# Attention scores in two fp32r parts, issued as pairs on the two row halves of the array

## The chip, the core and the metric

The kernel runs on one core of a Trainium2 chip. TensorE (PE; its weight loads appear as PEld) multiplies, VectorE (DVE), ScalarE (ACT) and GpSimd (POOL) work on the results, SyncE (SP) and ScalarE issue DMAs. The metric is the device time of one execution in microseconds; lower is better.

## The reference

Two layers, each used twice in turn, on x of 2048 rows by 512 columns: A is a Fourier mixing layer (two real DFTs as matmuls), B an attention in four segments of 512 positions with a running memory. B is where the change lies. Cut to what matters:

```python
q, k, v = x @ wq, x @ wk, x @ wv          # 32 heads of 16, segments of L = 512
for s in range(4):
    logits = einsum("bhqd,bhkd->bhqk", qs, ks) * scale + mask   # causal
    p = softmax(logits); a_dot = einsum("bhqk,bhkd->bhqd", p, vs)
    a_mem = (phi(qs) @ M) / (phi(qs) @ z + 1e-6)
    o = g * a_mem + (1 - g) * a_dot
    M, z = M + phi(ks).T @ vs, z + sum(phi(ks))
return concat(o) @ wo
```

## The kernel before, in words

The whole program is placed by hand on a line of slots: `place(order, generator, times)` puts one step of a generator into a slot, and a loop at the end runs the slots in order, within a slot by `order`. PE's matmuls keep that order on the chip. Times in slots, `t` for a unit's start.

**A unit** is four heads (HU) of one segment; a segment has eight, an attention 32, the program 64, and a unit's slots begin ten after those of the one ahead. One unit goes through these steps:

- `proj` (four slots, per group of eight heads) multiplies queries or keys into the bank `pqk` and splits them into parts, so that products of parts come near fp32. Before: three bf16 parts, by one ACT copy out of the bank, a POOL cast (L763), a POOL subtraction (L764), an ACT copy (L768) and a POOL subtraction (L772). Parts go by SP's queue (L781) to a scratch in DRAM, in six slots per head, so that query slot times key slot sums the six products of parts that matter.
- `stack` (slot t - 21) loads the slots of four heads back (L803), 96 rows high: `stkq` and `stkk`, with three more rows for the maxima (ones on the key side).
- `natural_max` (ten slots from t - 17) computes scores with queries on the partitions into banks called `nat` (L819 by way of the helper L82), one head at a time, 96 rows deep. DVE adds the mask and takes each row's maximum (L832). Four small DVE operations (L848 to L855) split the maxima into three bf16 parts.
- `max_rows` (slot t - 4): PE transposes the parts into the bank `mT`, ACT copies them out (`mt`, L870) and issues a DMA (L871) that writes them into the three extra rows of `stkq`.
- `softmax_values` (13 slots from t): the scores again, this time keys on the partitions and less the maxima, 99 rows deep, into banks `sT`. ACT clamps the diagonal (L900) and takes the exponential (L901) into `pT`; POOL zeroes what is above the diagonal (L904). In slot t + 12 the values are multiplied (`pv_bank`): four heads side by side on four column tiles of the array, 17 columns each.
- `output` (slot t + 14) transposes (`on`) and divides.

Score matmuls have 512, 384, 256 or 128 columns because of causality; per unit there are four of each for `nat` and four of each for `sT`. In every slot of the ten stand one bank of `sT` and one of `nat`, 512 columns each, and behind them in the same slot a step of a projection (`pqk`, `pvv`, `po`), of the memory (`pkT`, `pM`, `pm`) or a transpose. There are eight banks, one of which `pv_bank` keeps.

The other matmuls are fp32r with both operands split in two (`matmul3`), 128 rows by 512 columns, or plain fp32 (`pv`, `pM`, `pm`, which appear as two passes, and the transposes). PE loads weights for the next matmul while one runs.

The functions that the change touches:

Of the kernel before, what the change touches and what calls it, by code (L numbers as in the profile page):

```python
# [10 lines left out]
F32 = mybir.dt.float32  # L11
F32R = mybir.dt.float32r
# [44 lines left out]
def spectral_infini_kernel(  # L57
# [111 lines left out]
    def finish(ps, xr, x_out, i):  # L169
# [8 lines left out]
        consts.tile([P, MCOPIES, HU, LT], BF16, name=f"mparts{i}") for i in range(2)  # L178
# [500 lines left out]
    def place_attention(x_in, x_out, t0, w_at, out_at):  # L679
# [49 lines left out]
        def proj(s, g, n):  # L729
# [17 lines left out]
            parts = sb.tile([P, 3, 512], BF16, name="parts", bufs=2)  # L747
            with_phi = (n == "q" and s > 0) or (n == "k" and s < NSEG - 1)
            late = s == 0 and g < 2
            rem = sb.tile([P, 512], F32, name="rem", bufs=1)  # L750
            raw = sb.tile([P, 512], F32, name="praw", bufs=2) if with_phi else rem
# [11 lines left out]
            G.tensor_copy(parts[:, 0], raw)  # L763
            G.tensor_tensor(out=rem, in0=raw, in1=parts[:, 0], op=ALU.subtract)  # L764
# [3 lines left out]
            A.activation(parts[:, 1], rem, AF.Copy)  # L768
# [3 lines left out]
            G.tensor_tensor(out=parts[:, 2], in0=rem, in1=parts[:, 1], op=ALU.subtract)  # L772
# [3 lines left out]
            o = 0  # L776
            for a, cnt, step in SLOTS[n]:
                src = parts[:, a : a + cnt] if step else parts[:, a : a + 1].to_broadcast(
                    [P, cnt, 512]
                )  # L780
                nc.sync.dma_start(dst[:, o : o + cnt], src)  # L781
                o += cnt
# [7 lines left out]
        def stack(s, g, u):  # L790
            for n in "qk":
                number = (s * NG + g) * (HG // HU) + u
                if n == "q" or number < 3:
                    t = sb.tile(
                        [P, HU, 512], BF16, name=f"stk{n}", tag={"q": "chi", "k": "clo"}[n], bufs=3
                    )
                if n == "k" and number < 3:
                    G.memset(t[KROWS : KROWS + MROWS], 1.0)
# [11 lines left out]
        def natural_max(s, g, u):  # L810
# [3 lines left out]
            def scores(*cols):  # L814
                ps = bank("nat")
                views, off = [], 0
                for h, i in cols:
                    n = (i + 1) * P
                    T.matmul(  # L819
                        ps[:, off : off + n],  # L820
                        qs[:KROWS, h, i * P : (i + 1) * P],
                        ks[:KROWS, h, :n],
                        start=True,
                        stop=True,
                    )
                    views.append((ps[:, off : off + n], mx[:, h, i : i + 1]))
                    off += n
                for src, dst in views:
# [17 lines left out]
            rem = sb.tile([P, HU, LT], F32, name="mrem", bufs=2)  # L846
            with tc.high_priority(offset=2 * URGENT):
                V.scalar_tensor_tensor(  # L848
                    parts[:, 0], mx, -2.0, mx, op0=ALU.mult, op1=ALU.add
                )  # L850
                for dst in rem, parts[:, 1]:
                    V.scalar_tensor_tensor(
                        dst, mx, -1.0, parts[:, 0], op0=ALU.mult, op1=ALU.subtract
                    )
                V.scalar_tensor_tensor(  # L855
                    parts[:, 2], rem, 1.0, parts[:, 1], op0=ALU.mult, op1=ALU.subtract
                )
# [3 lines left out]
        def max_rows(s, g, u):  # L861
            qs, parts = stacks[s, g, u, "q"], maxima.pop((s, g, u))
            pt = bank("mT", (P, 2 * 512), BF16)
            T.transpose(
                pt[: MCOPIES * HU * LT, :P], parts.rearrange("p a h i -> p (a h i)"), ident_b
            )
            n = MROWS * HU * LT
            mt = sb.tile([P, P], BF16, name="mt", bufs=2)
            with tc.high_priority(offset=URGENT):
                A.activation(mt[:n], pt[:n, :P], AF.Copy)  # L870
            nc.scalar.dma_start(  # L871
                qs[KROWS : KROWS + MROWS].rearrange("p h s -> p (h s)"), mt[:n]
            )
            yield

        def softmax_values(s, g, u):
# [4 lines left out]
            def scores(dst, *cols):  # L881
                ps = bank("sT")
                off, diag = 0, []
                for h, kt in cols:
                    n = 512 - kt * P
                    T.matmul(
                        ps[:, off : off + n],
                        ks[:K, h, kt * P : (kt + 1) * P],
                        qs[:K, h, kt * P :],
                        start=True,  # L890
                        stop=True,
                    )
                    diag.append(off // P)
                    off += n
                blocks = ps.rearrange("p (b c) -> p b c", c=P)
                blocks = blocks[:, diag[0] : diag[-1] + 1 : max(1, diag[-1] - diag[0])]
                if x_out is out_tiles and (s * NG + g) * NU + u >= NSEG * USEG - 3 and cols[0][0] % 2:
                    V.tensor_scalar_max(blocks, blocks, 0.0)
                else:
# [442 lines left out]
```

## Time and profile before

| what | value |
|---|---|
| median of 3 runs | 1798.72 us (1797.68 to 1799.42) |
| span of the profiled execution | 1798.4 us |
| PE busy | 1742.2 us (97%) |
| DVE, ACT, POOL busy | 1405.3, 1110.9, 471.9 us |
| mean granted TensorE clock | 0.996 |
| attention stages | about 430 to 910 us and 1320 to 1798 us |

A row of a group gives the line, the engine, the operation, what is written and read, partitions by elements, the count, then busy time, the mean duration of one in ns, and the engine's idle time ahead of it with what ended it. A timeline row gives start and length in us. A matmul's length is from its start to its modelled end and overlaps with the next one; what PE needs for one is read from start to start. An fp32 matmul and its weight load are one instruction of the program, but appear as two in the trace.

### The profile page before, as it was taken

The numbers are of one execution on the slowest core, as the hardware profiler recorded it, in microseconds if no ns is written. First come the engines' busy times: TensorE is split into PE (matmuls) and PEld (weight loads), VectorE is DVE, ScalarE is ACT, GpSimd is POOL, SyncE is SP. The second block draws the span as 40 slices with busy tenths as digits, with TensorE's granted clock in tenths as the row PEclk, the third lists the DMA queues.
The fourth block names the chain that finished last, engine by engine and source line by source line (L and its number), as shares of the span: only waits on it lengthen the run. The fifth ranks groups of instructions, "written<-read, shape, count | busy, mean of one in ns | idle before, by whom it ended". The sixth has DMA issues, their size and how long they took to land.

```text
span 1798.4 us, 32155 instructions
## 1 busy us (share of the span) xinstructions
PE 1742.2 (97%) x10192; PEld 1257.4 (70%) x10192; DVE 1405.3 (78%) x4242; ACT 1110.9 (62%) x2391; POOL 471.9 (26%) x789
## 2 busy tenths in 40 slices
PE   8999999999999999998999999999998999999998
PEld 6888777877556666665568888888875666666654
DVE  8888978764887878877877997667658778787785
ACT  3344443432787878787773666444428887877785
POOL 1000000003453445454420000000134443544442
PEclk9999999999999999999999999999999999999999
DMA  8787775355453444433566777644546435344341
GB/s 289 239 277 236 250 230 170 113 166 169 142 161 109 156 128 129 150 116 122 165 199 213 265 231 238 195 154 142 167 143 185 129 118 160 117 145 140 104 131 42
DMA packets 169498, 302.81 MB, mean 168 GB/s; under 512 B 19568, under 2 KB 70768, under 8 KB 169328
## 3 DMA queue, kind: packets, MB, share of 16 engines
q1 hardware_dynamic: 159152, 287.39, 50.2%
q10 hardware_dynamic: 10176, 13.37, 2.1%
q8 instruction: 80, 1.31, 0.3%
q14 instruction: 90, 0.74, 0.1%
HBM read 211.83 MB, written 88.08 MB: 167 GB/s over the span
## 4 chain that ended last, share of the span: by engine, by line
PE 72%; DVE 11%; issue 2%; ACT 2%; DMA 1%; ACTq 0%; POOL 0%; DVEq 0%; SPq 0%
PE m L82 20%; PE pqk L82 9%; PE y L82 8%; PE pv_bank L82 8%; PE sT L82 7%; PE nat L82 6%; PE po L82 4%; PE pvv L82 4%; DVE junk L832 4%; DVE c L522 1%; PE pM L82 1%; PE pm L82 1%; PE on L82 1%; DVE clo L98 1%; ACT pT L901 1%
## 5 line engine op out<-in xcount | busy, mean ns | idle before, releaser
L832 DVE CUSTOM_DVE_ANT_0 junk<-nat,mask 128x512 bf16<-128x512 f32 (+3 forms) x1024 | 496.0, 484 | 143.2 <-PE nat L82 108.3
L901 ACT ACTIVATE pT<-sT 128x512 f32<-128x512 f32 x640 | 372.3, 599 | 18.1 <-ACT sT L900 4.7
L904 POOL TENSOR_SCALAR_AFFINE_SELECT pT<-pT 128x256 f32<-128x256 f32 (+1 forms) x448 | 201.8, 464 | 476.1 <-ACT pT L901 364.7
L82 PE MATMUL m<-chi,xa 128*128 128x512 f32 x1056 | 308.9, 393 | 2.9 <-DVE c L522 2.1
L82 PE MATMUL nat<-stkk,stkq 96*128 96x512 bf16 (+3 forms) x1024 | 244.5, 300 | 8.4 <-DVE mx L832 4.7
L82 PE MATMUL sT<-stkq,stkk 99*128 99x256 bf16 (+3 forms) x1024 | 248.8, 305 | 3.4 <-ACT pT L901 1.2
L900 ACT ACTIVATE sT<-sT 128x256 f32<-128x256 f32 (+1 forms) x628 | 205.2, 336 | 52.7 <-PE sT L82 47.2
L82 PE MATMUL m<-clo,xa 128*128 128x512 f32 x720 | 232.0, 394 | 5.1 <-DVE clo L98 5.1
L82 PEld LDWEIGHTS m<-chi,xa 128*128 128x128 f32 x1056 | 198.2, 188 | 46.0 <-DVE c L522 2.9
L82 PE MATMUL y<-wdt,us 128*128 128x512 f32 x768 | 182.3, 391 | 0.2 <-DVE wdt L98 0.2
L82 PEld LDWEIGHTS <-stkk 99*128 99x128 bf16 x1024 | 80.9, 98 | 134.2 <-issue 122.4
L82 PEld LDWEIGHTS y<-wdt,us 128*128 128x128 f32 x768 | 143.4, 188 | 30.5 <-DVE wdt L98 0.9
L82 PEld LDWEIGHTS m<-clo,xa 128*128 128x128 f32 x720 | 135.1, 188 | 37.3 <-DVE clo L98 9.6
L82 PE MATMUL pv_bank<-pT,v_all 128*17 128x512 f32 (+3 forms) x2048 | 153.6, 438 | 0.0
L96 ACT ACTIVATE chi<-cring 128x512 fp32r<-128x512 f32 (+1 forms) x138 | 99.6, 727 | 86.8 <-PE m L82 34.5
L145 POOL TENSOR_TENSOR r<-ve,half_neg 128x2 f32<-128x2 f32 (+2 forms) x24 | 19.3, 806 | 475.3 <-DVE ve L143 471.8
L82 PEld LDWEIGHTS <-stkq 96*128 96x128 bf16 x1024 | 94.1, 99 | 61.2 <-issue 20.2
L82 PE MATMUL pvv<-wv,xT 128*128 128x512 f32 x384 | 126.3, 440 | 3.7 <-DVE mx L832 3.7
L82 PE MATMUL pqk<-xT,wq 128*128 128x512 f32 x384 | 127.8, 442 | 0.0
L82 PE MATMUL po<-wo,oh 128*128 128x512 f32 x384 | 122.7, 435 | 0.9 <-ACT oh L96 0.5
L82 PE MATMUL pqk<-xT,wk 128*128 128x512 f32 x384 | 123.2, 430 | 0.0
L82 PEld LDWEIGHTS pv_bank<-pT,v_all 128*17 128x17 f32 x2048 | 54.0, 98 | 87.2 <-issue 83.0
(195 smaller groups left out, 2987.3 us busy)
## 6 DMA issues: line engine op xcount, KB each, us to landing
cring<-in_ct SPq DMA_DIRECT2D x97, 256.0 KB
stkq<-scrq SPq DMA_DIRECT2D x64, 384.0 KB
stkk<-scrk SPq DMA_DIRECT2D x64, 384.0 KB
cring<-sum SPq DMA_DIRECT2D x95, 256.0 KB
xt<-mid SPq DMA_DIRECT2D x64, 256.0 KB
cring<-in_ct SPq DMA_DIRECT2D x27, 512.0 KB
mid<-xr SPq DMA_DIRECT2D x48, 256.0 KB
scrq<-parts SPq DMA_DIRECT2D x32, 384.0 KB
```

Of the source, the lines that this page charges most:

```text
L82: return tc.keep_in_program_order(op(*args, **kwargs))
L96: pin(A.activation(hi, src, AF.Copy, scale=scale))
L98: lo_engine.tensor_tensor(out=lo, in0=src, in1=hi.bitcast(F32), op=ALU.subtract)
L145: G.tensor_tensor(out=r, in0=ve, in1=half_neg[:, :n], op=ALU.pow)
L522: V.tensor_tensor(out=dst, in0=c[tcn, base][:, m], in1=ps[m], op=op)
L832: last_max[0] = V.tensor_tensor_reduce(junk[:, :n], src, mask[:, 512 - n :], 1.0, 3e38, ALU.add, ALU.min, dst,)
L900: A.activation(blocks, blocks, AF.Relu)
L901: A.activation(dst, ps, AF.Exp, scale=-SCALE)
L904: G.affine_select(blocks, blocks, pattern=[[0, n] for n in blocks.shape[1:-1]] + [[1, P]], compare_op=ALU.is_ge, fill=0.0, base=0, channel ...
```

## The change

Queries and keys are split into two fp32r parts (the rounded value and the rest) and not three bf16 parts: three slots per head in the scratch, 48 rows in place of 96, and two rows of maxima in place of three, so 50 in place of 99. A stack now holds two heads in partitions 0 to 63 and two in 64 to 127. A score matmul of a head in the lower half and the same one of a head in the upper half are issued one behind the other, into two banks. The compiled program gives them a tile of 64 rows by 128 columns at row 0 and at row 64.

`natural_max` runs in five slots, two apart, in place of ten; `softmax_values` puts its `sT` pairs into the same five (t, t + 2, ... t + 8). So in every second slot stands a burst of four `sT` matmuls (or two of 512 columns) and as many `nat`, and in the slots between there are no scores. The last `nat` burst stands at t - 10 (before t - 8), the step on the maxima stays a slot or more behind (t - 8, before t - 7), `max_rows` stays at t - 4, `stack` moves to t - 22.

The first cut of the diff has the constants (a slot list now has part, first slot, count) and the splitting:

```diff
-SLOTS = {"q": ((0, 3, 0), (1, 2, 0), (2, 1, 0)), "k": ((0, 3, 1), (0, 2, 1), (0, 1, 1))}
-NSLOT = 6
+SLOTS = {"q": ((0, 0, 2), (1, 2, 1)), "k": ((0, 0, 1), (1, 1, 1), (0, 2, 1))}
+NSLOT = 3
 KROWS = NSLOT * DH
-MROWS = 3
+MROWS = 2
+SIDES = (0, 64)
+HP = 2
...
             A.activation(raw, ps, AF.Copy, scale=sign)
-            G.tensor_copy(parts[:, 0], raw)
-            G.tensor_tensor(out=rem, in0=raw, in1=parts[:, 0], op=ALU.subtract)
+            A.activation(parts[:, 0], ps, AF.Copy, scale=sign)
+            G.tensor_tensor(out=parts[:, 1], in0=raw, in1=parts[:, 0].bitcast(F32), op=ALU.subtract)
...
-            A.activation(parts[:, 1], rem, AF.Copy)
...
-            G.tensor_tensor(out=parts[:, 2], in0=rem, in1=parts[:, 1], op=ALU.subtract)
-            yield
-            sd = dram.tile([NSLOT, P, 512], BF16, name=f"scr{n}", bufs=3)
+            yield
+            sd = dram.tile([NSLOT, P, 512], F32, name=f"scr{n}", bufs=3)
```

The stacks, the scores for the maxima and the maxima:

```diff
-                last_stack[0] = nc.sync.dma_start(
-                    t[:KROWS].rearrange("p h s -> p (h s)"),
-                    src[:, u * HU * 512 : (u + 1) * HU * 512],
-                )
+                for a, at in enumerate(SIDES):
+                    first = (u * HU + a * HP) * 512
+                    last_stack[0] = nc.sync.dma_start(
+                        t[at : at + KROWS].rearrange("p h s -> p (h s)").bitcast(F32),
+                        src[:, first : first + HP * 512],
+                    )
...
             def scores(*cols):
-                ps = bank("nat")
+                banks = [bank("nat") for _ in SIDES]
                 views, off = [], 0
-                for h, i in cols:
+                for p, i in cols:
                     n = (i + 1) * P
-                    T.matmul(
-                        ps[:, off : off + n],
-                        qs[:KROWS, h, i * P : (i + 1) * P],
-                        ks[:KROWS, h, :n],
+                    for a, at in enumerate(SIDES):
+                        T.matmul(
+                            banks[a][:, off : off + n],
+                            qs[at : at + KROWS, p, i * P : (i + 1) * P],
+                            ks[at : at + KROWS, p, :n],
...
-            for h in range(HU):
-                scores((h, 3))
+            for p in range(HP):
+                scores((p, 3))
                 yield
-                scores((h, 0), (h, 2))
+                scores((p, 0), (p, 2))
                 yield
-                if h % 2:
-                    scores((h - 1, 1), (h, 1))
-                    yield
+            scores((0, 1), (1, 1))
+            yield
...
+                V.tensor_scalar(parts[:, 0], mx, -1.0, None, op0=ALU.mult)
                 V.scalar_tensor_tensor(
-                    parts[:, 0], mx, -2.0, mx, op0=ALU.mult, op1=ALU.add
-                )
-                for dst in rem, parts[:, 1]:
-                    V.scalar_tensor_tensor(
-                        dst, mx, -1.0, parts[:, 0], op0=ALU.mult, op1=ALU.subtract
-                    )
-                V.scalar_tensor_tensor(
-                    parts[:, 2], rem, 1.0, parts[:, 1], op0=ALU.mult, op1=ALU.subtract
+                    parts[:, 1], mx, -1.0, parts[:, 0].bitcast(F32), op0=ALU.mult, op1=ALU.subtract
                 )
...
-            nc.scalar.dma_start(
-                qs[KROWS : KROWS + MROWS].rearrange("p h s -> p (h s)"), mt[:n]
-            )
+            for a, at in enumerate(SIDES):
+                for r in range(MROWS):
+                    j = (r * HU + a * HP) * LT
+                    nc.scalar.dma_start(
+                        qs[at + KROWS + r : at + KROWS + r + 1].rearrange("p h s -> p (h s)").bitcast(F32),
+                        mt[j : j + HP * LT].bitcast(F32),
+                    )
```

`softmax_values` is changed in the same way (two banks, a loop over SIDES inside that over the columns, then clamp and exponential for each bank), with its three kinds of bursts at these slots, and the placement of the steps:

```diff
-                ev(6 + h, first)
+                ev(6 + 2 * p, first)
-                ev(2 + h, second)
+                ev(2 + 2 * p, second)
-                ev(h // 2, third)
+            ev(0, third)
...
-            place(1, natural_max(*unit(n)), run_from(t - 17, 10), [t - 7])
-            place(0.5, stack(*unit(n)), [t - 21])
+            place(1, natural_max(*unit(n)), run_from(t - 18, 5, 2), [t - 8])
+            place(0.5, stack(*unit(n)), [t - 22])
```

How this moves PE's instructions: here is PE before, from the end of one unit's values on (`stkk` and `stkq` are the stacks, `pm` reads the memory, `pqk` is a projection).

```order
L82 MATMUL pv_bank<-pT,v_all 17x512 x4
L82 MATMUL pv_bank<-pT,v_all 17x384 x4
L82 MATMUL pv_bank<-pT,v_all 17x128 x4
L82 MATMUL pv_bank<-pT_20107,v_all 17x256 x4
L82 LDWEIGHTS stkk
L82 MATMUL sT<-stkq,stkk 128x384
L82 LDWEIGHTS stkk
L82 MATMUL sT<-stkq,stkk 128x128
L82 LDWEIGHTS stkq
L82 MATMUL nat<-stkk,stkq 128x256
L82 LDWEIGHTS stkq
L82 MATMUL nat<-stkk,stkq 128x256
```

And PE after, at the same place:

```order
L84 MATMUL pv_bank<-pT,v_all 17x512 x4
L84 MATMUL pv_bank<-pT,v_all 17x384 x4
L84 MATMUL pv_bank<-pT,v_all 17x128 x4
L84 MATMUL pv_bank<-pT_18669,v_all 17x256 x4
L84 MATMUL sT<-stkq,stkk 128x384 x2
L84 MATMUL sT<-stkq,stkk 128x128 x2
L84 MATMUL nat<-stkk,stkq 128x512 x2
L84 MATMUL pm<-state_15711,phi 128x136 x2
L84 MATMUL pqk<-xT,wq 128x512 x3
L84 MATMUL sT<-stkq,stkk 128x384 x2
L84 MATMUL sT<-stkq,stkk 128x128 x2
L84 MATMUL nat<-stkk,stkq 128x128 x2
```

The weight loads of the scores are no longer instructions of their own, each score matmul has its partner behind it, and the projection that stood in every slot now stands between two bursts. Over the whole program the matmuls change between the array's three shapes (whole, 128 rows by 32 columns for `pv_bank`, 64 rows by 128 columns) 724 times, before 128 times.

The second place is ACT around the maxima of a unit. Before:

```order
L900 ACTIVATE sT<-sT 128x128
L870 ACTIVATE mt<-mT 48x128
L901 ACTIVATE pT<-sT 128x512
L871 DMA stkq<-mt 3x16x128
L900 ACTIVATE sT<-sT 128x128
L901 ACTIVATE pT<-sT 128x512
```

After:

```order
L900 ACTIVATE sT<-sT 128x128 x2
L864 ACTIVATE mt<-mT 32x128
L901 ACTIVATE pT<-sT 128x512 x2
L868 DMA stkq<-mt 1x8x128 x4
L900 ACTIVATE sT<-sT 128x128 x2
L901 ACTIVATE pT<-sT 128x512 x2
```

One issue of a DMA has become four, and ACT handles the banks of a pair together: two clamps, then two exponentials.

More of the change, by code (lines that the diff above doesn't have):

```diff
@@ L177, in spectral_infini_kernel @@
     max_parts = [
-        consts.tile([P, MCOPIES, HU, LT], BF16, name=f"mparts{i}") for i in range(2)
+        consts.tile([P, MCOPIES, HU, LT], F32R, name=f"mparts{i}") for i in range(2)
     ]
@@ L969, in last @@
                 pv(pb, 3, p1, 384)
-                pv(pb, 2, (p2[0][:, :2], p2[0][:, 2:]), 0)
+                pv(pb, 2, [p2[0][:, :, p] for p in range(HP)], 0)
                 ot = sb.tile([P, 512], F32, name="ot", tag="ut", bufs=8)
@@ L1287, in setup @@
         yield
-    ident = ident_b = mask = same_head = gate = None
+    ident = mask = same_head = gate = None
     def ones():
```

119 lines of the change are left out of this document (56 added, 63 removed).

## The prediction

> **What bounds the kernel now.** I read the page first: busy times, then the granted clock (full speed in all forty slices).
>
> ```profile
> span 1798.4 us, 32155 instructions
> PE 1742.2 (97%) x10192; PEld 1257.4 (70%) x10192; DVE 1405.3 (78%) x4242; ACT 1110.9 (62%) x2391; POOL 471.9 (26%) x789
> ```
>
> TensorE (PE) is busy for 97% of the span. Since the change touches only the attention stages, I read the busy time by windows there next: two stretches in the middle of an attention and two at an end.
>
> ```profile
> 600.00:700.00 100.00, 98.64 (x705) 64.04 (x707) 83.24 (x347) 79.39 (x188) 46.46 (x82) 1.00 0.42 134
> 1500.00:1600.00 100.00, 98.33 (x699) 64.04 (x698) 82.64 (x342) 81.52 (x195) 50.85 (x87) 1.00 0.40 124
> 800.00:880.00 80.00, 73.33 (x539) 44.30 (x537) 65.64 (x268) 62.13 (x148) 40.40 (x69) 0.96 0.47 147
> 1700.00:1798.40 98.40, 89.25 (x666) 53.16 (x664) 68.72 (x285) 67.66 (x161) 33.06 (x70) 1.00 0.28 87
> ```
>
> The columns are PE, PEld (weight loads), DVE, ACT and POOL. In the middle PE leaves 1.5 us of 100 free; DVE and ACT follow with about 83 and 80. At the ends PE waits for 7 to 9 us. So in most of the attention a microsecond of PE is a microsecond of time, and the question is what the new score matmuls cost PE, switching included.
>
> The profiled execution's span, 1798.4, is 0.3 us under the median of the runs, 1798.72, so the sum is made against the span and stands for both.
>
> **What the scores cost now.** The timeline of PE around two slots, and one long piece of the critical chain for the price of an ordinary fp32r matmul:
>
> ```profile
> 1225.46 31.96 PE y L82 x141
> 606.53 0.38 PE L82 MATMUL sT<-stkq,stkk 99*128 99x512 bf16 x1
> 606.75 0.38 PE L82 MATMUL nat<-stkk,stkq 96*128 96x512 bf16 x1
> 606.78 1.05 PE L82 MATMUL po<-wo,oh 128*128 128x512 f32 x3
> 610.21 0.39 PE L82 MATMUL sT<-stkq,stkk 99*128 99x256 bf16 x2
> 610.44 0.38 PE L82 MATMUL nat<-stkk,stkq 96*128 96x512 bf16 x1
> 610.47 1.04 PE L82 MATMUL pqk<-xT,wq 128*128 128x512 f32 x3
> 612.27 0.40 PE L82 MATMUL pqk<-xT,wq 128*128 128x512 f32 x1
> ```
>
> An fp32r matmul of 512 columns follows the next every 31.96/141 = 0.227 us. Three of them last 2 x 0.227 + 0.40 = 0.85. The three po end at 607.83, so without the scores they would have begun at 606.98: the scores in front of them took 606.98 - 606.53 = 0.45. The same for the second slot: 611.51 - 0.85 - 610.21 = 0.45; with about 0.01 for the hand-over from fp32r to bf16, 0.46 for 1024 columns. A unit (four heads) has ten such slots, 4.60 us, and there are 64 units: 294 us of PE time.
>
> **The pairs.** After the change two matmuls, on array rows 0-63 and 64-127, are issued one behind the other. What the trace has of tiles side by side is pv: four column tiles.
>
> ```profile
> 612.60 0.62 PE L82 MATMUL pv_bank<-pT,v_all 128*17 128x512 f32 x4
> 614.33 0.61 PE L82 MATMUL pv_bank<-pT,v_all 128*17 128x256 f32 x8
> 607.68 1.09 PE L82 MATMUL pM<-v_all,pkn 128*128 128x136 f32 x8
> 608.60 0.28 PE L82 MATMUL pm<-state,phi 128*128 128x136 f32 x1
> ```
>
> Four pv matmuls lie within 0.62, barely more than one, so a further tile costs some 0.007. No row shows row tiles, nor fp32r narrower than 512. I take pairs that run together, 0.22/512 us a column (sT to nat above), and 0.227 at 512: 0.234 for 512 columns, 0.179 for 384, 0.124 for 256. For 128 columns the stream would be 0.07, but each matmul needs its own fp32 weight load; eight pM matmuls with a load each, 0.28 long like the pm behind them, show a pace of (1.09 - 0.28)/7 = 0.116, so 0.116. A unit has four pairs of each width: 4 x 0.653 = 2.61 us. Saved: 64 x (4.60 - 2.61) = 127 us. Bounds: if the 128-column pair took twice its load (about what two fp32 passes of that width take, by the pace of pM), +0.116 x 4 x 64 = +30; if the load came faster, -0.05 x 4 x 64 = -13.
>
> **The switches.** These take it back. Entering and leaving a tiled mode:
>
> ```profile
> 612.60 0.13 PEld L82 LDWEIGHTS pv_bank<-pT,v_all 128*17 128x17 f32 x7 [0.37 <-issue]
> 931.08 0.40 PE L82 MATMUL pv_bank<-pT,v_all 128*17 128x256 f32 x4
> 931.40 0.50 PE L82 MATMUL m<-chi,xa 128*128 128x512 f32 x1
> 931.40 0.19 PEld L82 LDWEIGHTS m<-chi,xa 128*128 128x128 f32 x1 [0.42 <-issue]
> ```
>
> Into pv: the last pqk started at 612.27, pv at 612.60, 0.33 later where 0.227 is usual: 0.10 lost, and pv's load begins only then. Out of pv: the last group starts at 931.08, m at 931.40, 0.32 where the two groups at 614.33 are 0.61 - 0.40 = 0.21 apart: 0.11 lost. Here the fp32 load is not hidden either: it starts with its matmul, which lasts 0.50 and not 0.40, another 0.10 to 0.11. So a switch costs 0.10, and 0.11 more where a 128-column fp32 load stands behind it.
>
> The Trainium skill, "TensorEngine Tiling (Array Packing)", section Key Properties, says that changing the tiling mode, not just the tile, drains TensorE. By that rule row halves pay what pv pays, which the sum below takes; no run here shows a switch to row halves, so the other reading is a rival below.
>
> The order of PE's instructions, counted by tile size, has 128 switches before and 724 after: 331 into row halves, 327 out into the whole array, 66 into or out of pv. Added: 596 x 0.10 = +60. Loads bared: 331 entries x 0.11 = +36. Of the 327 exits 135 go to a transpose and 192 to a matmul.
>
> ```profile
> L82 PEld LDWEIGHTS m<-chi,xa 128*128 128x128 f32 x1056 | 198.2, 188 | 46.0 <-DVE c L522 2.9 <-DVE chi L98 1.5 <-ACT chi L96 0.5
> L82 PEld LDWEIGHTS on<-ident,ot 128*128 128x128 f32 x256 | 31.4, 140 | 2.4 <-ACT sT L900 0.5 <-ACT ot L972 0.3
> L82 PEld LDWEIGHTS <-stkq 96*128 96x128 bf16 x1024 | 94.1, 99 | 61.2 <-issue 20.2 <-PE nat L82 0.9 <-DMA stkk<-scrk 0.5
> 606.10 0.60 PE L82 MATMUL xnT<-ident,xn 128*128 128x128 f32 x4
> 606.42 0.27 PE L82 MATMUL xnT<-ident,xn 128*128 128x128 f32 x1
> ```
>
> A bf16 load lasts 99 ns, a transpose's 140, an fp32 matmul's 188; with the 188 costing 0.11 when bared, the 140 costs about 0.06: 192 x 0.11 + 135 x 0.06 = +29. The rows of xnT give a transpose's pace. The mT transpose turns from bf16 to fp32 and then costs what xnT does, (0.60 - 0.27)/3 = 0.11 in place of some 0.06: +3. PE's sum: -127 + 60 + 36 + 29 + 3 = +1. Halving the matmuls buys nothing if every burst pays for two switches.
>
> **Beside PE.**
>
> ```profile
> L848 DVE SCALAR_TENSOR_TENSOR mparts<-mx 128x16 bf16<-128x16 f32 x64 | 12.1, 188 | 1.1
> L855 DVE SCALAR_TENSOR_TENSOR mparts<-mrem,mparts 128x16 bf16<-128x16 f32 x64 | 15.3, 239 | 0.0
> L772 POOL TENSOR_TENSOR parts<-rem,parts 128x512 bf16<-128x512 f32 x64 | 76.0, 1187 | 28.2 <-ACT parts L768 26.9
> L871 ACTq DMA_DIRECT2D stkq<-mt x7: 728/729/755, 604.9 to 692.0; - x7
> L397 ACTq DMA_DIRECT2D sum<-cring x11: 326/326/354, 94.0 to 215.3; - x11
> PE mT L82 <- DVE mx L832: 6.8, 12, 3.0
> PE mT L82 <- DVE mparts L855: 4.8, 7, 0.9
> PE sT L82 <- DMA stkq<-mt: 0.7, 3, 0.3
> ```
>
> DVE loses two of four small operations per unit, 0.188 + 0.239 = 0.43 us, and the last scores of a unit are a slot further from mT. PE's waits at mT, 11.6 us in all, should halve: -5. POOL loses a cast and a subtraction per projection, one of 1.19; hidden under PE, since PE works through projections and y when the first units start: 0. One ACT queue issue of 0.73 turns into four. Their patterns are plain ones, nearest to the 0.33 of sum: 1.30, +0.57 per unit. A unit lasts (692.0 - 604.9)/6 = 14.5, of which ACT is busy for 11.5, so it is hidden: 0; at 0.73 each it is +2.2, and ACT is full (the bound above). PE waits for that DMA only 0.7 us in the run, so the later landing is hidden too. Three of the four also wait for the DMA eight before them, whose completion semaphore they take over; behind them in ACT's queue stand the next relu and exp, and behind those PE's next burst, which needs the banks. That DMA was mostly issued half a unit earlier, so I take 0 and keep it for a rival. Stack loads turn from two SP issues into four, the writes of the parts from six to five per group; bytes stay. Two banks taken at once for sT and two for nat, in place of one each: the number per unit stays, the bursts are twice as high; -0 to +0.2 per unit, taken as 0. The six memsets of the key stacks become twelve, at the start only: 0.
>
> Sum: 1798.4 + 1 - 5 = **1794 us**, by itself 1776 to 1815.
>
> **Rivals.**
> *Cheap switches.* Row halves are picked per instruction and loads go ahead. For it: only column tiles show the drain. If the drain stays but loads are hidden: -127 + 60 + 3 - 5 = -69, 1730. If nothing is paid, PE frees 1.9 us a unit, and ACT, 11.5 + 0.73 + 0.57 = 12.8 of 14.5, takes over near 1700; half the slack lost, 1745. I say 1735. Against it: the load that waited at 931.40.
>
> *Loads in turn* (slower). The two halves' loads share one path. Then a pair takes at least 2 x 0.116 = 0.232: a unit has 4 x (0.234 + 3 x 0.232) = 3.72, +71, and each entry bares a second load, +36: some 1900. It decides once loads of two halves follow each other by more than 0.06. Against it: seven pv loads begin within 0.13 us. The skill's "TensorE: Matmul & The Clock Gate", section LDWEIGHTS, says that load time goes by columns, whatever the rows, so half the rows would not be loaded faster; no run shows it. Pairs that don't overlap at all belong here as well and cost more.
>
> *ACT or banks become the bound* (slower). Four issues of 0.73, or ACT stuck behind a DMA slot, fill ACT's 14.5; the bursts then wait for banks: +0.4 a unit, taken as half of one such issue, 1824. Against it: ACT's 79 of 100, which leave 3 us a unit.
>
> **How the numbers follow.** A measurement here tells 0.2%, 3.6 us, from no change. Forecast 0.50 (of it faster 0.24, same 0.09, slower 0.17); cheap switches 0.28; loads in turn or no overlap 0.12; ACT or banks 0.10. Faster 0.24 + 0.28 = 0.52, same 0.09, slower 0.17 + 0.22 = 0.39. The range goes from 1725 to 1850: it leaves out the last rival above (0.12) and the lower end of cheap switches (0.07).
>
> **What would show it.** Right: sT and nat pairs start 7 ns apart, the first matmul after a burst starts about 0.2 late with its load beside it, a group of scores with its switches takes what two slots take now, 0.92. Wrong: loads of sT that begin before the matmul ahead has ended (cheap switches), 128-column pairs 0.23 apart (loads in turn), or PE idle before sT released by ACT.

## The result, and the profile after

The changed kernel takes 2060.78 us (median of 4 runs, 2052.54 to 2065.61), the kernel before 1799.07 beside it: ratio 1.145, 95% interval 1.142 to 1.148, slower by 262 us. The profiled execution has a span of 2050.8 us, 252.4 more than before.

The page of the changed kernel: span, busy times, the granted clock in forty slices.

```profile
span 2050.8 us, 32671 instructions
PE 1854.5 (90%) x10192; PEld 1308.2 (64%) x10192; DVE 1390.6 (68%) x4116; ACT 1079.4 (53%) x2388; POOL 356.0 (17%) x667
PEclk9999999998899989998899999999988999899878
```

And its row in the list of cores:

```profile
core 0: 2050.8 us, clock 0.940
```

PE is busy 112.3 us longer for the same number of matmuls, and idle 140.1 us longer (196.3 in place of 56.2); together that is the 252.4. The clock, at full speed throughout before, is down in both attentions. A mean of 0.940 is (1 - 0.940) x 2 x 2050.8 = 246 us at half speed, which costs up to 123 us of PE work: the longer busy time. The waits that bear on it (us in all, times, longest), PE's, ACT's and DVE's:

```profile
PE sT L84 <- DMA stkq<-mt: 139.3, 70, 4.4
ACT sT L900 <- DMA stkq<-mt: 67.5, 33, 3.0
DVE junk L834 <- PE nat L84: 362.8, 166, 11.3
```

And the DMA's group among the instructions on that tile (shortest, median and longest issue in ns):

```profile
L868 ACTq DMA_DIRECT2D stkq<-mt x256: 627/627/1237, 453.1 to 2020.9; - x128
```

PE's wait at `sT` for the maxima's rows was 0.7 us before; ACT now waits behind its own issues, and DVE for the late scores. One issue takes 0.63 us, and four with the gaps between them 2.63 to 2.7. One unit shows the whole of it. ACT's timeline, SP's, PE's, and the busy time by windows:

```profile
702.87 0.25 ACT L864 ACTIVATE mt<-mT 32x128 fp32r<-32x128 f32 x1
703.15 0.63 ACTq L868 DMA_DIRECT2D stkq<-mt  x1
703.82 0.63 ACTq L868 DMA_DIRECT2D stkq<-mt  x1
704.48 1.29 ACTq L868 DMA_DIRECT2D stkq<-mt  x2
705.83 0.43 ACT L900 ACTIVATE sT<-sT 128x128 f32<-128x128 f32 x2 [1.23 <-DMA stkq<-mt]
```

```profile
704.32 0.96 SPq L803 DMA_DIRECT2D stkq<-scrq  x2
705.32 1.27 SPq L803 DMA_DIRECT2D stkk<-scrk  x2
```

```profile
706.08 0.38 PE L84 MATMUL sT<-stkq,stkk 50*128 50x256 f32 x1
709.11 0.76 PE L84 MATMUL sT<-stkq,stkk 50*128 50x256 f32 x3 [2.65 <-DMA stkq<-mt]
713.08 3.52 PE L84 MATMUL pv_bank<-pT,v_all 128*17 128x512 f32 x32
```

```profile
704.00:709.00 5.00, 2.46 (x13) 1.47 (x11) 2.24 (x9) 3.53 (x9) 2.21 (x4) 0.97 0.86 239
709.00:712.00 3.00, 2.90 (x11) 2.41 (x12) 1.63 (x7) 2.15 (x5) 0.06 (x1) 0.50 0.79 270
712.00:716.00 4.00, 4.00 (x27) 1.22 (x30) 1.35 (x5) 0.00 (x0) 0.58 (x1) 0.56 0.00 0
716.00:720.00 4.00, 4.00 (x42) 2.73 (x32) 2.33 (x9) 3.32 (x9) 0.77 (x2) 1.00 0.00 0
```

The fourth issue ends at 705.77. From 704.32 on, 1.17 us after the first issue began, SP issues four stack loads of another unit, 192 KB each. The upper half's first `sT` starts at 709.11, 3.3 us after that issue (the landing, as this text calls it: from the end of the last issue until the reader goes on), having waited 2.65. Then the clock (the column after the five engines) is at half for some 6 us, while PE works without a gap. ACT's next clamp stood 1.23 us behind the issues.

Before, the DMA of the maxima's rows in one of the tightest units in the middle of an attention looked like this (ACT, then SP):

```profile
678.73 0.73 ACTq L871 DMA_DIRECT2D stkq<-mt  x1
```

```profile
681.48 0.30 SPq L803 DMA_DIRECT2D stkq<-scrq  x1
```

The stack loads came 2.75 us after the start of the one issue and 2.0 us after its end. After the change they fall between the issues: four issues take longer than one, and the first load starts 1.17 us after the first issue and not 2.75.

### The profile page after: what moved, and what is told of

The parts are those of the page before. It is cut to its first block, busy times and chain, and to the rows that moved or that the text cites. A ratio compares the mean times of both kernels' runs of the same rounds, so it can differ in the third digit from the quotient of the medians.

```text
span 2050.8 us, 32671 instructions
## 1 busy us (share of the span) xinstructions
PE 1854.5 (90%) x10192; PEld 1308.2 (64%) x10192; DVE 1390.6 (68%) x4116; ACT 1079.4 (53%) x2388; POOL 356.0 (17%) x667
## 4 chain that ended last, share of the span: by engine, by line
PE 33%; DMA 5%; ACT 5%; DVE 3%; ACTq 2%; issue 2%; POOL 0%; DVEq 0%
PE m L84 13%; DMA stkq<-mt 5%; PE pv_bank L84 5%; PE y L84 4%; PE pqk L84 3%; ACT pT L901 2%; PE sT L84 2%; PE po L84 2%; ACTq L868 2%; PE pvv L84 1%; PE nat L84 1%; DVE junk L834 1%; ACT sT L900 1%; PE oT L84 0%; PE on L84 0%
## 5 line engine op out<-in xcount | busy, mean ns | idle before, releaser
L901 ACT ACTIVATE pT<-sT 128x512 f32<-128x512 f32 x640 | 350.0, 606 | 5.7 <-DMA stkq<-mt 5.0
L84 PE MATMUL sT<-stkq,stkk 50*128 50x256 f32 (+3 forms) x1024 | 191.1, 390 | 157.5 <-DMA stkq<-mt 139.3
L904 POOL TENSOR_SCALAR_AFFINE_SELECT pT<-pT 128x256 f32<-128x256 f32 (+1 forms) x448 | 193.2, 445 | 771.4 <-ACT pT L901 622.8
L900 ACT ACTIVATE sT<-sT 128x256 f32<-128x256 f32 x625 | 179.6, 329 | 191.4 <-PE sT L84 117.4
L84 PEld LDWEIGHTS sT<-stkq,stkk 50*128 50x128 f32 x1024 | 99.3, 195 | 283.8 <-issue 144.4
L84 PE MATMUL pv_bank<-pT,v_all 128*17 128x512 f32 (+3 forms) x2048 | 188.4, 515 | 0.0
L84 PE MATMUL nat<-stkk,stkq 48*128 48x512 f32 (+3 forms) x1024 | 168.3, 358 | 3.0 <-DVE mx L834 1.8
L966 ACT ACTIVATE ot<-pv_bank 128x512 f32<-128x512 f32 x64 | 38.2, 598 | 195.2 <-PE pv_bank L84 195.2
L84 PEld LDWEIGHTS nat<-stkk,stkq 48*128 48x128 f32 x1024 | 110.6, 202 | 20.0 <-issue 5.7
L84 PE MATMUL pqk<-xT,wk 128*128 128x512 f32 x384 | 113.5, 425 | 0.8 <-ACT parts L764 0.7
```

The source lines that it names most:

```text
L84: return tc.keep_in_program_order(op(*args, **kwargs))
L900: A.activation(blocks, blocks, AF.Relu)
L901: A.activation(dst[a], ps, AF.Exp, scale=-SCALE)
L904: G.affine_select(blocks, blocks, pattern=[[0, n] for n in blocks.shape[1:-1]] + [[1, P]], compare_op=ALU.is_ge, fill=0.0, base=0, channel ...
L966: A.activation(ot, pb, AF.Copy)
```

## The experiments

The theory: the four issues end late, the rows then land behind the stack loads (*late rows*), ACT's queue stands still meanwhile (*ACT stuck*), and gaps on PE halve the clock. The main rival: pairs, switches and bared loads (weight loads that no matmul covers) cost PE more than the sum had. Each ratio is to the kernel before measured beside the run (medians from 1794.9 to 1800.2 us).

| run | rows: issues, queue, slot; other | us (ratio, 95% interval) | clock | PE's wait at sT for rows |
|---|---|---|---|---|
| changed | 4, ACT, t - 4 | 2060.8 (1.142 to 1.148) | 0.940 | 139.3 |
| 1 | 4, ACT, t - 7 | 1909.2 (1.060 to 1.065) | 0.977 | none |
| 2 | 4, SP, t - 4 | 1879.2 (1.043 to 1.050) | 0.983 | 40.1 |
| 3 | 2, ACT, t - 4 | 1869.4 (1.037 to 1.045) | 0.975 | 40.5 |
| 4 | 4, ACT, t - 4; sT reads no rows | 1884.4 (1.047 to 1.052) | 0.984 | none |
| 5 | before, 4, ACT, t - 4 | 1889.8 (1.048 to 1.052) | 0.980 | 36.0 |
| 6 | 2, ACT, t - 5 | 1817.3 (1.009 to 1.012) | 0.989 | 1.4 |
| 7 | 2, SP, t - 5 | 1796.3 (0.998 to 1.000) | 0.994 | 1.0 |
| 8 | as 3, both halves the same | 1943.9 (1.078 to 1.082) | 0.988 | 9.4 |
| 9 | as 7, nat behind the step | 1860.7 (1.032 to 1.037) | 0.993 | 0.9 |
| 10 | 2, SP, t - 6 | 1798.8 (0.999 to 1.001) | 0.994 | 0.8 |
| 11 | 4, SP, t - 6 | 1809.2 (1.005 to 1.009) | 0.992 | 4.6 |
| 12 | before, 1, SP, t - 4 | 1796.0 (0.997 to 1.000) | 0.996 | 1.2 |
| 13 | as changed, stacks at t - 21 | 2049.4 (1.136 to 1.141) | 0.944 | 138.2 |
| 14 | as changed, stacks at t - 20 | 2041.5 (1.133 to 1.137) | 0.946 | 130.9 |
| 15 | as changed, few stack loads | 1880.9 (1.044 to 1.049) | 0.983 | 30.1 |

**1. The rows three slots earlier.**

```diff
-[t - (5 if x_out is out_tiles and n == NSEG * USEG - 1 else 4)]
+[t - 7]
```

> The changed kernel with the maxima's rows (transpose, copy, four issues) three slots earlier: t - 7 in place of t - 4, nothing else. Theory (late rows: four issues of 0.63 us one behind the other, then some 3 us of landing, end 2 to 3 us after PE asks for them, and each such gap also halves TensorE's clock for some us): three slots are some 4.4 us, more than the lateness, so PE's wait at sT for that DMA falls from 139 us to under 20, the mean clock goes from 0.94 to 0.99 and the time to 1790 to 1840 us. Rival (the pairs, switches and bared loads cost PE more than the sum had): PE stays busy for 1850 us, only the wait can go, not under 1920. Rival (the DMAs' completion slots hold ACT up): ACT still waits for those DMAs by some 60 us and the time stays above 1950.

The wait for rows is gone, but the time is 70 us over the theory's range. The rows were not all: ACT's clamps still wait behind the four issues, 37.4 us in all. Run 11 below issues the same four DMAs from SP, one slot later than this run, and takes 1809.2: with the rows early in both, 100 us lie between ACT's queue and SP's.

**2. The four issues on SP's queue.**

```diff
-                    nc.scalar.dma_start(
+                    nc.sync.dma_start(
```

> The changed kernel with the four issues of the maxima's rows on SP's queue in place of ACT's. Theory (late rows, by the number of issues and the landing): SP issues them as serially, so the last lands about as late as now; only what stood behind them in ACT's queue (two clamps and two exponentials, 2.7 us later per unit) is freed: part of the 252 us comes back, 1880 to 2000 us. Rival (ACT's queue is the cause, the rows only late because ACT is): nearly all comes back, 1800 to 1840. Rival (SP's stack loads and part writes stand in front of the rows): slower than 2061.

1879 is 1 us under the theory's range: more came back than it had for ACT's queue. But the move also changed the landing. On SP's queue the stack loads stand behind the rows (the first starts 0.1 us after the fourth issue), and where PE waits for the rows, it now starts 1.27 us after that issue, in unit after unit.

**3. Two issues.** The parts of the maxima lie in the order side, part, head, so that both rows of a side go at once:

```diff
-                for r in range(MROWS):
-                    j = (r * HU + a * HP) * LT
-                    nc.scalar.dma_start(
-                        qs[at + KROWS + r : at + KROWS + r + 1]...
+                j = a * MROWS * HP * LT
+                nc.scalar.dma_start(
+                    qs[at + KROWS : at + KROWS + MROWS]...
```

> The changed kernel with the maxima's parts in the order side, part, head, so that the two rows of a side go in one DMA: two issues in place of four. Theory (late rows, by the number of issues): the last one is issued 1.3 us sooner, of 2 to 3 us that it is late: the wait at sT falls from 139 to 40 to 80 us, the clock to 0.96 to 0.98, the time to 1880 to 1960 us. If the landing of some 3 us alone is the cause, whatever the number: above 2000. If the pairs and switches are the cause: 2040 to 2061, less 64 x 1.3 = 83 us of ACT time that costs nothing.

1869: more than the 1.3 us of issue time were worth in the theory. The clamps' wait behind the issues, 67.5 us, is gone: the two exponentials ahead of the clamp last 1.1 us and cover two issues, not four.

**4. No wait for the rows.**

```diff
-            K = KROWS + MROWS
+            K = KROWS
```

> The changed kernel with sT matmuls 48 rows deep in place of 50, so that they don't read the maxima's rows and don't wait for them; the four DMAs are still issued. It leaves out the subtraction of the maxima (the exponential's factor is divided by 1024 so that nothing overflows). It shows PE's own sum for pairs, switches and loads, with ACT's issues beside it. Theory (late rows): 1790 to 1830 us, clock 0.99. Rival (pairs, switches and loads cost more than the sum had): 1900 or more with the clock at 0.99. Rival (ACT's queue with four issues is the bound): 1850 to 1950, PE waiting for banks or at pv_bank for pT.

1884: outside the theory's range (up to 1830) and inside that of the rival on ACT's queue (1850 to 1950), which is right here. ACT's wait in all, and one unit of its timeline:

```profile
ACT sT L900 <- DMA stkq<-mt: 71.3, 35, 2.8
```

```profile
711.62 2.63 ACTq L868 DMA_DIRECT2D stkq<-mt  x4
714.30 0.43 ACT L900 ACTIVATE sT<-sT 128x128 f32<-128x128 f32 x2 [2.71 <-DMA stkq<-mt]
```

The clamp and its exponential start when the fourth issue is out. PE then waits more for banks: at `nat` for those that DVE's maxima free, 14.2 us in all (run 7, whose issues are on SP: 1.4). How the late clamp passes on to these banks is not shown step by step. Against the 1794.9 us of the kernel before beside it the issues alone cost some 89 us, and the wait for the rows the other 172 to 176, by which of the two measurements of the kernel before is taken.

**5. Four issues in the kernel before.**

```diff
-            nc.scalar.dma_start(
-                qs[KROWS : KROWS + MROWS].rearrange("p h s -> p (h s)"), mt[:n]
-            )
+            for r, h, c in ((0, 0, 2), (0, 2, 2), (1, 0, HU), (2, 0, HU)):
+                j = (r * HU + h) * LT
+                nc.scalar.dma_start(
+                    qs[KROWS + r : KROWS + r + 1, h : h + c]..., mt[j : j + c * LT]
+                )
```

> The kernel before with its one issue of the maxima's rows cut into four (first row in two halves, second, third), on ACT's queue and in the same slot; nothing else. Theory (the four issues are the cause): ACT's queue is taken 4 x 0.65 in place of 0.73 us per unit, the next clamp and exponential stand behind it, and the last row lands 2 us later. The kernel before left the row 1.5 to 5 us between the end of the issue and the first sT, so in a part of the units PE waits for rows or banks: 0.5 to 2 us per unit, 1830 to 1930 us, with PE's wait at sT at 10 us or more (now 0.7). Rival (pairs, switches and bared loads cost more than the sum had, the issues are hidden): 1793 to 1805.

The middle of the theory's range: 91 us slower without a single pair on row halves or switch to them.

```profile
PE sT L82 <- DMA stkq<-mt: 36.0, 20, 4.8
```

Two units of this run show how long the rows take to land. In the first, SP's stack loads start 0.04 us after the fourth issue ends (579.30); in the second they start within the issues:

```profile
578.01 1.29 ACTq L873 DMA_DIRECT2D stkq<-mt  x2
579.34 0.30 SPq L803 DMA_DIRECT2D stkq<-scrq  x1
580.59 0.38 PE L82 MATMUL sT<-stkq,stkk 99*128 99x256 bf16 x2 [0.36 <-DMA stkq<-mt]
```

```profile
868.03 2.86 ACTq L873 DMA_DIRECT2D stkq<-mt  x4
870.23 0.33 SPq L803 DMA_DIRECT2D stkq<-scrq  x1
874.52 0.59 PE L82 MATMUL sT<-stkq,stkk 99*128 99x256 bf16 x2 [2.90 <-DMA stkq<-mt]
```

`sT` starts 1.29 us after the last issue in the first and 3.63 in the second. So loads that start behind the last issue don't delay the rows, and loads that start ahead of it do. In most units between the ends of an attention they start behind it here, which is why PE's wait for rows is 36 us in this run and 139 in the changed kernel.

**6 and 7. Two issues as in run 3, a slot earlier, on ACT and on SP (the second change is run 7's alone).**

```diff
-[t - (5 if x_out is out_tiles and n == NSEG * USEG - 1 else 4)]
+[t - 5]
...
-                nc.scalar.dma_start(
+                nc.sync.dma_start(
```

> Two issues in place of four, as in the run before, and the rows one slot earlier (t - 5). That run left 40 us of PE's wait at sT (33 times) and a clock of 0.975. Theory (what is left are still late rows, and the clock that they cost): one slot is 1.45 us, the wait falls to under 15 us, the clock to 0.985, the time to 1825 to 1850. Rival (what is left is ACT's queue, stuck for 1.3 us per unit, or the bursts on two banks): 1860 or more.

> As the run ahead of it (two issues, t - 5) with the issues on SP's queue in place of ACT's. Theory (ACT's queue stuck behind issues is the other half of the loss): ACT is free of 1.3 us per unit, 1800 to 1830 us. Rival (SP's queue: rows stand behind stack loads and part writes and land later): PE's wait at sT rises again, 1850 or more. If ACT's queue doesn't matter: the same as the run ahead of it within 5 us.

1817 and 1796: both better than the theory's range. With rows early and ACT's queue free the changed kernel is level with the one before (0.998 to 1.000) and 2 us from the forecast.

```profile
PE 1754.0 (98%) x10192; PEld 1261.0 (70%) x10192; DVE 1384.6 (77%) x4116; ACT 1074.7 (60%) x2388; POOL 359.0 (20%) x667
```

**8. Both matmuls of a pair on the same half.**

```diff
-                            qs[at : at + KROWS, p, i * P : (i + 1) * P],
-                            ks[at : at + KROWS, p, :n],
+                            qs[:KROWS, p, i * P : (i + 1) * P],
+                            ks[:KROWS, p, :n],
```

and the same in `sT`.

> Two issues (t - 4), and both matmuls of a pair on the array's lower row half: the second reads the lower heads' stacks again, so the upper heads' scores are wrong (left out: their real values). Switches, loads, banks and DMAs stay. It shows what running side by side is worth. By the prediction's prices a unit's pairs last 4 x 0.65 = 2.6 us side by side, and one behind the other 8 x (0.227 + 0.17 + 0.12 + 0.11) = 5.0: +2.4 us per unit, +154, less what late rows hide behind it (up to 40): 1985 to 2030 us. If pairs did not run together: within 15 us of 1869.

+75 in place of +116 to +161: below the range. The run it is compared with (3) still lost time to late rows, which PE's longer work now covers (40.5 to 9.4 us), and to the clock (0.975 to 0.988); how much of the shortfall these two make up was not measured. The pace shows without that. A burst of four `sT` and four `nat` of 256 columns, first in pairs (run 7), then on one half (run 8):

```profile
713.13 0.50 PE L84 MATMUL sT<-stkq,stkk 50*128 50x256 f32 x4
713.47 0.40 PE L84 MATMUL nat<-stkk,stkq 48*128 48x256 f32 x4
713.80 0.96 PE L84 MATMUL po<-wo,oh 128*128 128x512 f32 x3
```

```profile
702.94 0.74 PE L84 MATMUL sT<-stkq,stkk 50*128 50x256 f32 x4
703.52 0.64 PE L84 MATMUL nat<-stkk,stkq 48*128 48x256 f32 x4
704.09 1.20 PE L84 MATMUL pqk<-xT,wq 128*128 128x512 f32 x4
```

0.34 and 0.33 against 0.58 and 0.57: on one half four matmuls take 4 x 0.118, in pairs two do, and 0.11 (the bared load) or 0.10 (the drain on leaving) comes on top in both. Over eight units in the middle of the first attention, from one unit's first `pv_bank` to the ninth one's, for before, run 7, run 8 and run 9:

```profile
580.07 0.62 PE L82 MATMUL pv_bank<-pT,v_all 128*17 128x512 f32 x4
698.92 0.62 PE L82 MATMUL pv_bank<-pT,v_all 128*17 128x512 f32 x4
```

```profile
580.32 0.62 PE L84 MATMUL pv_bank<-pT,v_all 128*17 128x512 f32 x4
698.53 0.62 PE L84 MATMUL pv_bank<-pT,v_all 128*17 128x512 f32 x4
```

```profile
601.27 0.62 PE L84 MATMUL pv_bank<-pT,v_all 128*17 128x512 f32 x4
737.36 0.62 PE L84 MATMUL pv_bank<-pT,v_all 128*17 128x512 f32 x4
```

```profile
589.08 0.62 PE L84 MATMUL pv_bank<-pT,v_all 128*17 128x512 f32 x4
718.35 0.62 PE L84 MATMUL pv_bank<-pT,v_all 128*17 128x512 f32 x4
```

118.9, 118.2, 136.1 and 129.3 us. Running side by side is worth (136.1 - 118.2)/8 = 2.24 us a unit; the expectation had 2.4. (Runs 7 and 8 also differ in the rows' queue and slot, but in these stretches PE is idle for under 0.5 us in both, at full clock.)

**9. More switches.**

```diff
-            place(1, natural_max(*unit(n)), run_from(t - 18, 5, 2), [t - 8])
+            place(2.5, natural_max(*unit(n)), run_from(t - 18, 5, 2), [t - 8])
```

> Two issues on SP's queue at t - 5 (the run with 1796 us), and in every slot the nat pairs stand behind the slot's other step in place of ahead of it, so most bursts split in two. PE then changes tile size 1190 times in place of 720: 238 more entries into row halves and 232 more exits. It prices the switches. By the prediction's terms: 470 x 0.10 + 238 x 0.11 + 232 x 0.09 = 47 + 26 + 21 = +94, so 1890 us, with 1865 to 1905 allowed for slack. Rival (cheap switches, or the mode costs nothing): 1796 to 1815.

+64 in place of +94, 4 us under the range; the rival of cheap switches is out. In the eight units PE changes tile size 75 times more, and (129.3 - 118.2)/75 is 0.15 per change, where the prices said 0.20. The rows still show 0.10 and 0.11. Part of the difference is that in run 7 the second `nat` of a pair often waits for its bank (105 pairs more than 20 ns apart, 24.5 us in all; run 9: 32 pairs, 9.9 us): nat behind the step gives the bank time. That is 15 of the 30 us; the rest stays open.

**10 to 12. How early, how many, and the kernel before with the same mending.** Run 10 is run 7 at `[t - 6]`; run 11 is the changed kernel's four issues as `nc.sync.dma_start` at `[t - 6]`; in run 12 the edit is to the kernel before:

```diff
-            nc.scalar.dma_start(
+            nc.sync.dma_start(
                 qs[KROWS : KROWS + MROWS].rearrange("p h s -> p (h s)"), mt[:n]
```

> Two issues on SP's queue, one slot earlier still (t - 6). Theory (rows already early enough at t - 5, PE is the bound at 98% busy): 1788 to 1800 us, no difference from 1796 by over 6 us. Rival (some rows still late at t - 5 in the units at the ends): under 1788. Rival (the transpose now waits for the maxima): over 1800, with PE waiting at mT.

> The changed kernel's four issues on SP's queue at t - 6. Theory (what counts is that nothing stands behind the issues on ACT and that the last row lands before PE asks): the number no longer matters, 1790 to 1806 us. Rival (the number of small DMAs itself, through completion slots or the engines): 1815 or more.

> The kernel before with its one issue on SP's queue, same slot: what the mending alone gives without the change. Theory (hidden there, ACT has 3 us a unit free, PE waits 0.7 us in all for the rows): 1790 to 1800 us, no difference. Rival (ACT's queue cost something before too): 1775 to 1788. Rival (SP's queue delays the rows): over 1805, PE waiting at sT.

1798.8 (no difference), 1809.2 (3 us over the theory's range; 4.6 us of wait for rows are left) and 1796.0. So once the issues start early and not on ACT, their number matters little: some 10 us between four and two. No version beats the kernel before by more than a measurement tells: run 7's interval holds 1, and run 12's gain of 0.16% (0.05 to 0.27) is not the change's.

**13 and 14. Stack loads later.** `[t - 22]` becomes `[t - 21]`, then `[t - 20]`.

> The changed kernel with the stack loads one slot later (t - 21, where the kernel before had them), nothing else. Theory (the rows land late because 768 KB of stack loads are issued between the first and the last of the four row issues): the loads come some 1.5 us later, for about half of the units behind the rows; there the rows land 1.3 us after the last issue in place of 3.0 to 4.3, PE's wait at sT falls from 139 to 40 to 90 us, the time to 1930 to 2000 us; ACT's queue stays stuck, so not below 1880. Rival (the landing has to do with the small DMAs or with ACT's queue): the wait stays above 110 us and the time above 2020.

> As the run ahead of it, two slots later (t - 20), so that nearly all loads follow the rows. Theory: the rows land 1.3 us after the last issue in nearly all units, PE's wait at sT falls under 50 us; what is left is ACT's queue: 1880 to 1950 us, less sure since the first nat at t - 18 may now wait for its stacks. Rival (small DMAs or ACT's queue): above 2020.

By their times and waits (138.2 and 130.9 us) both fall on the rival, that the landing has to do with the small DMAs or with ACT's queue. But neither tests it: the edit hardly moved what it was to move (the runs are 11 and 19 us faster than the changed kernel). In run 14's trace the loads are issued where they were, in the midst of the four (ACT's timeline, SP's, and what SP waits for):

```profile
701.45 0.63 ACTq L868 DMA_DIRECT2D stkq<-mt  x1
702.78 1.29 ACTq L868 DMA_DIRECT2D stkq<-mt  x2
```

```profile
702.61 0.96 SPq L803 DMA_DIRECT2D stkq<-scrq  x2
```

```profile
SPq L803 <- PE nat L84: 223.0, 53, 14.5
```

SP's queue had long come to them and waited for PE: a load needs the stack that the last burst of the unit ahead reads. Their time is set by that burst, not by the slot in which the loads are placed.

**15. Hardly any stack loads.**

```diff
-                if n == "q" or number < 3:
+                if number < 3:
...
-                for a, at in enumerate(SIDES):
+                for a, at in enumerate(SIDES[: 2 * (number < 3)]):
```

(the three query stacks are kept as the key stacks are)

> The changed kernel with stack loads for the first three units of each attention alone; the later units work on those stacks again (left out: their real queries and keys), the four row issues stay on ACT at t - 4. Theory (the rows land late because the stack loads are issued in their midst): without loads the rows land 1.3 us after the last issue, PE's wait at sT falls from 139 to 30 to 70 us and the time to 1890 to 1970 us; ACT's queue stays stuck for 2.7 us per unit, so not below 1860. Rival (four small DMAs from ACT land late by themselves): the wait stays above 110 us, the time above 2020.

1881 is 9 us under the theory's range, and the wait at its lower edge; the rival (above 2020) is out. PE's wait, and a unit's row of ACT and of PE:

```profile
PE sT L84 <- DMA stkq<-mt: 30.1, 40, 1.9
```

```profile
585.24 2.66 ACTq L869 DMA_DIRECT2D stkq<-mt  x4
```

```profile
589.17 0.47 PE L84 MATMUL sT<-stkq,stkk 50*128 50x256 f32 x3 [0.58 <-DVE onat L1034]
```

The last issue ends at 587.90, and the second half's `sT` starts 1.27 us later. In units 9 to 24 of the first attention (counted from 0) the last wait of a unit ended 3.0 to 4.3 us after the last issue in the changed kernel, and here 1.27 to 1.29 wherever PE waited. The four issues are the same, so the 1.7 to 3 us are time behind the loads. In some units at the ends of the attentions the wait still ended 2.1 to 2.7 us after the last issue in this run; in two of them (units 3 and 6) SP issues writes of the parts up to just before that issue ends.

The Trainium skill, "DMA: Bandwidth & Descriptors", section Issuing engines are not separate DMA queues, says that DMAs from ScalarE and SyncE run on the same 16 engines and interleave. The traces agree: 1.27 us with the loads out of the way, 3.0 to 4.3 behind them.

## Why the prediction was wrong, point by point

*The steps that failed.* "Their patterns are plain ones, nearest to the 0.33 of sum: 1.30, +0.57 per unit. ... so it is hidden: 0." One issue takes 0.63, near the other end given (0.73), so four hold ACT's queue for 2.63 to 2.7 us. ACT's idle time, 3 us a unit, was no cover: what counts is who stands behind those issues, and that is the clamp on which PE's next bank hangs. Run 4 puts it at 89 us, and run 11, which differs from run 1 in the queue and one slot, is 100 us faster than run 1. "PE waits for that DMA only 0.7 us in the run, so the later landing is hidden too": that 0.7 is how much PE waited, not how much room there was. What counts is whether the last issue is out before the first stack load starts. In units 9 to 24 of the first attention of the kernel before, that load starts 2.75 to 4.6 us after the issue of the rows starts, so one issue of 0.73 is out in time, and even four, 2.6 us, are (run 5 in its middle units). In the changed kernel it starts 0.7 to 2.6 us after the first of four issues. So the room shrank too, which the prediction doesn't mention: the load waits for the last `sT` burst that reads its stack, and the change moves that burst from slot t + 9 to t + 8, while the rows stay at t - 4. The times are measured; that this slot is the reason is read from the placement, and no run tests it alone. Rows that are issued among the loads then land 1.7 to 3 us later, behind up to 768 KB. That is worth 180 us (run 15), gaps and halved clock together; what run 15 leaves, 83 us over the kernel before beside it, is about what run 4 has for ACT's queue. Run 5 has the four issues in the kernel before, with the loads where they were: 91 us slower, with 36 us of PE's wait for rows in place of 139.

*The clock* was no term at all. The Trainium skill, "TensorE: Matmul & The Clock Gate", Part 1, says that an idle window of about 3.4 us halves the clock and a busy one of that length brings it back. The trace agrees that it halves (0.50 in the window above), but 2.65 us without work were enough (1.42 in the next unit, followed by 3.4 us at half), and here the clock took some 6 us of work to come back.

*The rival that came nearest*, ACT or banks as the bound, had the right place and the slower sign, with 0.4 us a unit for the first link (89/64 = 1.4 by run 4) and nothing for the landing and the clock. Its sign, PE idle before `sT` released by ACT, is not what came: 139.3 us of its waits there ended with the DMA. Nor was ACT stuck behind DMA slots: in 58 of the 64 units the four issues go out in 2.63 to 2.7 us. So even the range stopped at 1850. (Its 1824 is added to the span and not to the sum, 4 us too much, and the rival of 0.12 that the range leaves out is loads in turn, which is not the last one in the list.)

*The steps that held.* With the rows issued early and from SP (run 7) the time is 1796.3, where the sum said 1794; eight undisturbed units take 118.2 in place of 118.9 us, where the sum had -0.5. The pairs: in the trace of after the two of a pair start 1 to 4 ns apart, their loads too, and

```profile
700.06 0.94 PE L84 MATMUL pqk<-xT,wq 128*128 128x512 f32 x3
700.93 0.50 PE L84 MATMUL sT<-stkq,stkk 50*128 50x512 f32 x2
701.27 0.40 PE L84 MATMUL nat<-stkk,stkq 48*128 48x512 f32 x2
```

the third pqk starts at 700.60, the sT pair 0.33 later (0.227 and 0.10 of drain), the nat pair 0.34 behind it (0.227 and 0.11 of bared load). Loads in turn is out by the same rows, cheap switches by run 9. Mis-sized by little: 128-column pairs take 0.06 and not 0.116, which the second nat's waits for banks, taken as 0, give back (4 x 64 x 0.056 = 14 us against 24.5 in run 7). That the sum is met within 2 us is thus luck in part. PE's waits for the maxima at mT fell from 11.6 to 4.1 us (the sum: -5).

*Left open*: the half of run 9's shortfall, part of run 8's, and why run 1 with its rows at t - 7 is still 25 us slower than run 4, which reads none.

## What to carry to other kernels

Before a DMA is split into several, read not how long its reader waits but how much room it has in the tightest unit: what other transfers start there, and whether the change moves them. Here a small DMA that slipped in among 768 KB of loads was 1.7 to 3 us late, and one issued just ahead of them was not late at all. Issues on an engine's queue are to be priced by who stands behind them, not by the engine's idle time: a queue with no compute behind it (here SP's) took two of them at no cost that shows (runs 7 and 10). And a gap on a matmul-bound kernel can be paid nearly twice, here as 140 us of idle time and as 112 us of longer work at half clock.

## What the runs showed of the hardware

Issue time did not go by size: 0.63 us for one row of 4 KB, 0.62 for two rows, 8 KB together (run 7), 0.73 before for three rows, 12 KB together, and 0.41 for a stack load of 192 KB in the changed kernel. Pairs of fp32r matmuls on the two row halves run fully side by side, 128-column ones at 0.06 us a pair, half the time that a whole-array 136-column one with its own load takes. And a run whose clock is at half for 12% of its span (246 of 2051 us) has no wait longer than 4.4 us at its `sT`: many short ones are enough.
